# A decode block's forward and backward kernel: its instruction order planned anew, with landing times of all transfers in flight renewed at each issue

## The chip, the cores and the metric

The kernel runs on one core of a Trainium2 chip. The metric is the device time of one execution in microseconds (us); lower is better. The time before is the median of five runs.

## What is computed

The reference is a decode step (one token, batch 2) of grouped-query attention over a cache plus a bilinear gated MLP, and its gradients by `jax.vjp`. Cut to what matters:

```python
B, D, Hq, Hkv, Sk, Dh, F = 2, 576, 32, 16, 4096, 128, 4608
xn = layernorm(x)
q = (xn @ wq).reshape(B, 1, Hq, Dh)                    # each K/V head serves 2 query heads
p = softmax(q @ k_cache^T * Dh ** -0.5)                # per head, over 4096 positions
attn = (p @ v_cache).reshape(B, 1, Hq * Dh) @ wo
mlp = ((xn @ w_gate) * (xn @ w_up)) @ w_down
out = x + attn + mlp
outputs: out, and the gradients for x, k_cache, v_cache, wq, wo, w_gate, w_up, w_down
```

All arrays are bfloat16. With one token, every gradient of a cache or a weight is an outer product: it is as large as the cache or the weight itself and has to be written in full. The caches are 64 heads-by-batch pieces of 1 MB to read, and their gradients 64 pieces of 1 MB to write.

## The kernel before

The work has 16 steps. A step `s` is one group of two K/V heads (`g = s // 2`, eight groups) for one of the two batch rows. Beside the steps there are nine slices of 512 columns of the MLP (`mlp`, L666 ff.).

- **Cache loads** (`load_kv`, L926, on SP's queue): four a step, K then V for two heads, 1 MB each, into nine buffers `kv`.
- **Turning** (`turn`, DVE, L357): each cache buffer is transposed in 32x32 blocks into one of three buffers `X`, two instructions of 1024 columns each.
- **Group front** (`group_front`): L787 multiplies w_q of the group with the normalised token (20 matmuls: four heads of four 128-row blocks and one small block, which comes in a transfer of its own, L940); L820 does the same for w_o and the incoming gradient. `rep` (L804) carries the result to POOL, which builds the stationaries `W` (L1001) of the steps.
- **Attention** (`softmax`, `dscore`): scores (L1036, 32 matmuls per head), softmax with row maximum and sum through small matmuls, then `spread` (L1048, L1054), whose copy to `pp` or `dd` is what the next stages read.
- **Outer products** (`head_outer`, L1069): `BD`, a block-diagonal form of the query or gradient made by POOL (L1024, 32 times), times `pp` or `dd`. Two matmuls fill a PSUM buffer `o` (three of them); an eviction on ACT (L361) or DVE (L363) casts 128x1024 values into a stage buffer `st` (four of them). Four evictions make one 1 MB piece of a cache gradient, which SP stores (L583). `BIAS` tilts the choice between ACT and DVE.
- **Contraction** (`contract`, L1209): p with V and dscore with K from the untransposed buffers, in four parts; after the last the four `kv` buffers of the step are free for the next loads.
- **Group back** (`group_back`) after two steps: the gradients of w_q and w_o, again outer products through `st`, stored from POOL's queue (L583), with `tl` for the last 64 rows.
- **MLP slice**: loads of w_gate and w_up (POOL L959, small parts SP L962) and w_down (SP L966), then its products and three gradients stored from POOL.

Every engine runs its instructions in the order in which they stand, and so do the two queues from which transfers are issued, SP's and POOL's: an instruction that waits holds all that stands behind it. That order isn't written by hand. Each part of the work is a generator that yields what it needs (an engine for so long, a buffer of a ring, an event, a transfer); the class `Order` keeps a clock per engine with costs written in the source, and takes, among the parts that could start within `SLACK` of the earliest on an engine, the one with the lowest priority number (`PR`, with `HEAD` for steps 0 and 1 and `TAIL` for steps 14 and 15, plus `STEP` per step). The instructions are emitted in the order so found. The class `Lines` is its model of the transfers: two lines, SP's and POOL's, that share the transfer rate by packet size; `push` adds a transfer and says when it will land. Weights are loaded when a certain count of cache loads has been issued: `8*g + WQ0` and `8*g + WO0` for w_q and w_o, `MLP0 + i*MLPD` for the slices.

The clock of `Order` exists only while the program is built. On the chip, waits are semaphores that follow from what is read and written.

Of the kernel before, what the change touches and what calls it, by code (L numbers as in the profile page):

```python
# [31 lines left out]
        self.land = None  # L32


class Lines:
    def __init__(self):
        self.now, self.line = 0.0, ([], [])

    def work(self, line, until):
        while self.now < until and (line[0] or line[1]):  # L40
            busy = [q for q in line if q]
            total = sum(q[0][1] for q in busy)
            step = min(min(q[0][0] * total / q[0][1] for q in busy), until - self.now)
            for q in busy:
                q[0][0] -= step * q[0][1] / total
                if q[0][0] < 1e-9:
                    q.pop(0)
            self.now += step

    def push(self, k, at, work, packet):  # L50
        self.work(self.line, at)
        if not (self.line[0] or self.line[1]):
            if at > self.now + 0.3:
                work += DRY
            self.now = max(self.now, at)
        self.line[k].append([work, packet])
        now, line, n = self.now, tuple([list(x) for x in q] for q in self.line), len(self.line[k])
        while line[k]:
            self.work(line, self.now + 1e-6 + min(q[0][0] for q in line if q))
        end, self.now = self.now, now  # L60
        return end


class Order:
# [44 lines left out]
    def start(self, s):  # L109
        r = s.req  # L110
        if r[0] == "op":
            return max(s.ready, self.free[r[1]]), r[1]
        if r[0] == "any":
            best = None
            for e, cost, bias in r[1]:
                t = max(s.ready, self.free[e])
                if best is None or t + cost + bias < best[0]:
                    best = (t + cost + bias, t, e)
            return best[1], best[2]
        if r[0] == "wait":  # L120
            if any(e.t is None for e in r[1]):
                return None, None
            return max([s.ready] + [e.t for e in r[1]]), None
        if r[0] == "acq":
            ts = [t for t in self.slots[r[1]].values() if t is not None]
            if not ts:
                return None, None
            return max(s.ready, min(ts)), None
        if r[0] == "dma":
            return max(s.ready, self.free[r[1]]), r[1]  # L130
        if r[0] == "gate":
            if r[2] < 0:
                return s.ready, None
            e = r[1][min(int(r[2]), len(r[1]) - 1)]
            return (None, None) if e.t is None else (max(s.ready, e.t), None)
        raise ValueError(r)

    def run(self):
        while self.streams:
            cand = []  # L140
            for s in self.streams:
                t, e = self.start(s)
                if t is not None:
                    cand.append((t, s.prio, s, e))
            assert cand, "no stream can go on: %s %s" % (
                [(x.gen.__name__, x.gen.gi_frame.f_lineno, x.ready, x.req) for x in self.streams], self.slots)
            t, _, s, e = min(cand, key=lambda c: c[:2])
            if e is not None:
                t, _, s, e = min((c for c in cand if c[3] == e and c[0] <= t + SLACK[e]), key=lambda c: (c[1], c[0]))
            r = s.req  # L150
            value = None
            if r[0] in ("op", "any"):
                cost = r[2] if r[0] == "op" else next(c for x, c, _ in r[1] if x == e)
                quad = r[3] if len(r) > 3 else None
                if quad is not None and self.quad == (1 - quad, t):
                    cost = 0.12
                self.free[e] = t + cost
                if e == "PE":
                    self.quad = (quad, t + cost)
                s.ready = t + cost + self.HOP  # L160
                self.log.append((t, cost, e, s.gen.__name__))
                value = e
            elif r[0] in ("wait", "gate"):
                s.ready = t
            elif r[0] == "acq":
                slots = self.slots[r[1]]
                i = min((k for k, v in slots.items() if v is not None), key=lambda k: (slots[k], k))
                slots[i] = None
                s.ready = t
                value = i  # L170
            elif r[0] == "dma":
                self.free[e] = t + r[2]
                s.land = self.lines.push(e == "POOL", t + r[2] + LATENCY[e], r[3], r[4]) + 1.4
                s.ready = t + r[2]
                self.log.append((t, r[2], e, s.gen.__name__))
            self.advance(s, value)
# [34 lines left out]
def WAIT(*events):  # L211
    return ("wait", events)


def SET(event):
    return ("set", event)
# [10 lines left out]
def DMA(engine, cost, nbytes, row=8192):  # L227
# [3 lines left out]


NKV, NX, NGU, NWW, NST, NBD = 9, 3, 1, 5, 4, 3
MLP0, MLPD = 7, 4.12
KVSTORE = "SP"
WQ0, WO0 = -6, 0
LATENCY, DRY = {"SP": 0.6, "ACT": 0.6, "POOL": 2.0}, 0.4
BIAS = 0.37
SLACK = {"PE": 0.05, "ACT": 0, "DVE": 0, "POOL": 4.39, "SP": 3.25}
STEP = 28.0  # L240
HEAD = {"turn0": 37.0, "turn1": -35.7, "att": -22.4, "dsc": 17.6, "con": -15.0, "out0": 23.5, "front": 20.5, "back": 16.6, "W1": -1.0, "BD1": 2.3, "BD0": -12.8, "load": -30.3}
TAIL = {"turn0": -15.1, "att": -22.9, "dsc": -43.3, "con": 54.4, "out1": 30.2, "back": -0.9, "W0": 22.3, "W1": 12.9, "BD1": 41.5, "BD0": 93.7, "load": 0.2}
PR = {"turn0": 171.8, "turn1": 90.3, "att": 19.2, "dsc": -129.0, "con": 69.0, "out1": 42.8, "out0": 77.7, "front": -89.9,
      "back": 17.7, "W0": -47.7, "W1": 227.7, "BD1": -2.0, "BD0": -48.1, "mlp": -78.9, "wout": 54.1, "store": 33.6,
      "load": 262.3, "wload": -168.7, "fin": -1.5, "const": 62.9, "mload": 371.2}


def pr(name, s):
# [5 lines left out]
def kernel(  # L254
# [33 lines left out]
    NS = NG * Bq  # L288
# [281 lines left out]
    class Store:  # L570
        def __init__(self, n, out, prio):
            self.n, self.out, self.prio = n, out, prio
# [197 lines left out]


    grp = [dict(Lm=Event(), Eq=Event(), Ed=Event(), Lq=Event(), Lo=Event()) for _ in range(NG)]
    steps = [dict(done=Event(), outs=[Event(), Event()], sm=Event(), dsv=Event()) for _ in range(NS)]

    def group_front(g):
        st = grp[g]
# [323 lines left out]
    def softmax(s):  # L1100
# [47 lines left out]
        yield REL("m", m)  # L1148
        yield SPAWN(outer(s, 1, "pp", S["pp"], pp_t[S["pp"]][:, 1]), pr("out1", s))
        S["ppT"] = pp_t[S["pp"]][:]  # L1150

    def dscore(s):
        S = steps[s]
# [41 lines left out]
    def contract(s):  # L1195
        S = steps[s]
        g, b = divmod(s, Bq)
        if b == 0:
            grp[g]["oT"] = yield ACQ("oT")
        oT = oT_t[grp[g]["oT"]]  # L1200
        yield WAIT(S["sm"], Ezero)
        m = yield ACQ("m")
        ct = m_t[m]
        heads = [(S["ppT"], kvS[s][1][l], l) for l in range(G)] + [(S["ddT"], kvS[s][0][l], l) for l in range(G)]
        for part in range(4):
            yield PE(0.95)
            for c in range(8 * part, 8 * part + 8):
                for j, (rT, slot, l) in enumerate(heads):
                    nc.tensor.matmul(ct[32 * j:32 * j + 32, 0:P], lhsT=view(rT, 0, P, 4 * c + 2 * l, [[1, 32]]),  # L1209
                                     rhs=kv_t[slot][:, Dh * c:Dh * (c + 1)], start=(c == 0), stop=(c == NCH - 1))  # L1210
        for t in range(2):
            for l in range(G):
                yield REL("kv", kvS[s][t][l])
        i = yield ACQ("osb")
        e = yield EV(128)
        if e == "ACT":
            nc.scalar.activation(osb_t[i][:], ct[:, 0:P], AF.Copy, scale=oscale[:])
        else:
            nc.vector.tensor_scalar(osb_t[i][:], ct[:, 0:P], oscale[:], None, op0=ALU.mult)
        yield REL("m", m)  # L1220
        m = yield ACQ("m")
        yield PE(0.3)
        nc.tensor.matmul(m_t[m][:, 0:8], lhsT=osb_t[i][:], rhs=view(ident[:], 0, P, 0, [[32, 4], [1, 2]]),
                         start=True, stop=True)
        yield REL("osb", i)
        yield DVE(0.19)
        nc.vector.tensor_copy(view(oT[:], 0, P, b, [[GH * 32, 2], [32, GH]]),
                              m_t[m][:, 0:8].rearrange("p (t h) -> p t h", t=2))
        yield REL("m", m)
        yield SET(S["done"])  # L1230
# [148 lines left out]
```

## Time and profile before

| what | value |
|---|---|
| median of five runs | 513.48 us (509.31 to 515.99) |
| the profiled execution: its own time, its span | 513.48 us, 511.7 us |
| instructions | 19318 |
| PE, DVE, ACT, POOL busy | 377.1, 372.1, 305.2, 228.1 us |
| moved by DMA | 186.19 MB, half read and half written |
| mean granted TensorE clock | 0.667 |

The page gives busy time per engine; the span in 40 slices of 12.8 us, where a digit is the busy share in tenths; the queues; the chain of work that ended last; groups of instructions with their mean duration and the idle time before them. Line numbers are those of the kernel before. Waits name the instruction that waited and the one that released it. A DMA share of 1.00 in a stretch means that the core's 16 DMA engines were busy throughout it.

### The profile page before, as it was taken

The numbers are of one execution on the slowest core, as the hardware profiler recorded it, in microseconds if no ns is written. First come the engines' busy times: TensorE is split into PE (matmuls) and PEld (weight loads), VectorE is DVE, ScalarE is ACT, GpSimd is POOL, SyncE is SP. The second block draws the span as 40 slices with busy tenths as digits, with TensorE's granted clock in tenths as the row PEclk, the third lists the DMA queues.
The fourth block names the chain that finished last, engine by engine and source line by source line (L and its number), as shares of the span: only waits on it lengthen the run. The fifth ranks groups of instructions, "written<-read, shape, count | busy, mean of one in ns | idle before, by whom it ended". The sixth has DMA issues, their size and how long they took to land.

```text
span 511.7 us, 19318 instructions
## 1 busy us (share of the span) xinstructions
PE 377.1 (74%) x8506; PEld 246.9 (48%) x8506; DVE 372.1 (73%) x657; ACT 305.2 (60%) x463; POOL 228.1 (45%) x323
## 2 busy tenths in 40 slices
PE   0629848878787888597787776678588875896976
PEld 0417535645455464445456443444455563563544
DVE  6739958789665788769683984659776775897883
ACT  5025837575673758284783746447466664867783
POOL 6147534447424545446334362416551462256411
PEclk9997757585655667756765965557655666966775
DMA  7994889999998999999999899967999999899885
GB/s 275 402 370 185 328 327 367 409 409 407 410 397 351 341 379 374 392 420 420 393 401 411 297 417 408 412 264 295 396 377 408 410 380 385 345 378 325 341 336 215
DMA packets 34235, 186.19 MB, mean 364 GB/s; under 512 B 4156, under 2 KB 6344, under 8 KB 17768
## 3 DMA queue, kind: packets, MB, share of 16 engines
q1 hardware_dynamic: 22224, 141.25, 69.8%
q0 software_dynamic: 11920, 43.72, 22.4%
q8 instruction: 66, 1.08, 0.8%
q14 instruction: 17, 0.14, 0.1%
q10 hardware_dynamic: 8, 0.00, 0.0%
HBM read 92.48 MB, written 92.48 MB: 361 GB/s over the span
## 4 chain that ended last, share of the span: by engine, by line
PE 33%; DMA 33%; issue 11%; DVE 10%; ACT 9%; POOL 3%; SPq 1%; ACTq 0%; DVEq 0%; POOLq 0%
DMA out_dram<-st 23%; ACT st L361 8%; PE ps_o L1069 7%; PE ps_m L1209 6%; PE ps_m L1036 6%; DMA ww<-in_A_wq_dram 5%; DVE X L357 5%; DMA gu<-in_B_w_up_dram 4%; DVE st L363 2%; PE ps_m L820 2%; PE ps_o L603 2%; PE ps_m L679 1%; POOL BD L1024 1%; PE ps_o L617 1%; SPq L926 1%
## 5 line engine op out<-in xcount | busy, mean ns | idle before, releaser
L361 ACT CAST st<-ps_o 128x1024 bf16<-128x1024 f32 (+1 forms) x290 | 258.9, 946 | 124.0 <-DMA out_dram<-st 62.1
L357 DVE STREAM_TRANSPOSE X<-kv 128x1024 f32<-128x1024 f32 x128 | 154.7, 1223 | 9.9 <-PE ps_m L1036 5.0
L1024 POOL TENSOR_TENSOR BD<-vr,mask 128x2048 bf16<-128x2048 bf16 x32 | 115.2, 3599 | 43.7 <-PE ps_o L1069 24.2
L363 DVE CAST st<-ps_o 128x1024 bf16<-128x1024 f32 (+1 forms) x86 | 99.3, 1158 | 42.7 <-DMA out_dram<-st 18.8
L583 POOL DMA_DIRECT2D out_dram<-st x43 | 33.2, 772 | 99.3 <-ACT st L361 69.7
L1069 PE MATMUL ps_o<-BD,pp 32*128 32x512 bf16 x256 | 51.9, 521 | 23.2 <-ACT st L361 22.9
L1036 PE MATMUL ps_m<-X,W 128*32 128x128 bf16 x2048 | 62.8, 292 | 5.9 <-issue 2.1
L1209 PE MATMUL ps_m<-kv,pp 128*32 128x128 bf16 x1024 | 56.9, 279 | 9.4 <-issue 9.3
L1069 PE MATMUL ps_o<-BD,dd 32*128 32x512 bf16 x256 | 54.8, 512 | 9.8 <-ACT st L361 6.0
L1209 PE MATMUL ps_m<-kv,dd 128*32 128x128 bf16 x1024 | 56.6, 279 | 3.1 <-issue 3.1
L1036 PEld LDWEIGHTS <-W 128*32 128x32 bf16 x2048 | 48.2, 130 | 19.7 <-issue 15.5
L1209 PEld LDWEIGHTS <-pp 128*32 128x32 bf16 x1024 | 44.2, 126 | 15.5 <-issue 14.7
L1209 PEld LDWEIGHTS <-dd 128*32 128x32 bf16 x1024 | 44.0, 126 | 8.8 <-issue 8.8
L1001 POOL COPY W<-rep 32x16 bf16<-32x16 bf16 x128 | 24.6, 192 | 47.2 <-DVE rep L804 31.7
L357 DVE STREAM_TRANSPOSE X<-ww 128x1152 f32<-128x1152 f32 x25 | 34.3, 1371 | 5.9 <-PE ps_m L1036 3.2
L1069 PEld LDWEIGHTS <-pp 32*128 32x128 bf16 x256 | 11.2, 98 | 41.6 <-issue 38.1
L1069 PEld LDWEIGHTS <-dd 32*128 32x128 bf16 x256 | 13.0, 98 | 26.2 <-issue 21.7
L554 POOL COPY wt<-wm 64x128 bf16<-64x128 bf16 (+1 forms) x34 | 8.9, 260 | 31.0 <-DVE wm L548 30.0
L583 POOL DMA_DIRECT2D out_dram<-tl x26 | 14.5, 561 | 18.0 <-ACT tl L361 9.8
L357 DVE STREAM_TRANSPOSE X<-gu 128x1024 f32<-128x1024 f32 x18 | 22.0, 1227 | 0.3 <-PE ps_m L1036 0.3
L787 PE MATMUL ps_m<-xs,ww 128*128 128x2 bf16 x160 | 5.7, 165 | 15.7 <-DMA ww<-in_A_wq_dram 8.4
L603 PEld LDWEIGHTS <-xnr 32*128 32x128 bf16 x416 | 12.9, 119 | 7.2 <-issue 6.1
(202 smaller groups left out, 526.0 us busy)
## 6 DMA issues: line engine op xcount, KB each, us to landing
out_dram<-st SPq DMA_DIRECT2D x64, 1024.0 KB
kv<-in_A_k_cache_dram SPq DMA_DIRECT2D x32, 1024.0 KB
kv<-in_A_v_cache_dram SPq DMA_DIRECT2D x32, 1024.0 KB
out_dram<-st POOLq DMA_DIRECT2D x26, 512.0 KB, 7.2
out_dram<-st POOLq DMA_DIRECT2D x17, 576.0 KB, 9.5
ww<-in_B_w_down_dram SPq DMA_DIRECT2D x9, 576.0 KB
ww<-in_A_wo_dram POOLq DMA_DIRECT2D x8, 576.0 KB, 10.5
gu<-in_B_w_gate_dram POOLq DMA_DIRECT2D x9, 512.0 KB, 11.3
```

Source lines behind the costliest of these rows:

```text
L357: nc.vector.transpose(out, in_)
L361: nc.scalar.copy(out, in_)
L363: nc.vector.tensor_copy(out=out, in_=in_)
L554: nc.gpsimd.tensor_copy(view(Wt[:], 64 * h, 64, 0, [[dims[-1][1], n], [1, dims[-1][1]]]), view(Wm[:], 64 * h, 64, off, dims))
L583: (nc.gpsimd if engine == "POOL" else nc.sync).dma_start(dst, src)
L603: nc.tensor.matmul(o[:, aa, dc * P:(dc + 1) * P], lhsT=xnr[32 * a:32 * a + 32, dc * P:(dc + 1) * P], rhs=rhs(a), start=True, stop=True)
L820: nc.tensor.matmul(dp, lhsT=Wdy[:, e, 2 * k:2 * k + P], rhs=view(X[:], 0, P, 64 * k + e, [[D, GH], [2, 32]]), start=(k == 0 and e == 0), s ...
L1001: nc.gpsimd.tensor_copy(view(W_t[t][w][:], 32 * a, 32, 6 + 8 * a, [[G * WW, 4], [WW, G], [1, 2]]), view(rep_t[grp[g]["qs"]][:], 32 * a, 32 ...
L1024: nc.gpsimd.tensor_tensor(BD_t[i][:], view(vr_t[v][:], 0, P, 0, [[0, 16], [1, Dh]]), view(mask16[:], 0, P, 0, [[1, 16], [0, Dh]]), ALU.mult)
L1036: nc.tensor.matmul(sc[32 * cq:32 * cq + 32, :], lhsT=view(W[:], 0, P, (be * G + l) * WW + 6 - 4 * c2 - 2 * l, [[1, 32]]), rhs=view(X[:], 0 ...
L1069: nc.tensor.matmul(o[:, k, :], lhsT=pr2[32 * c4:32 * c4 + 32, :], rhs=BD[32 * c4:32 * c4 + 32, 8 * l + 4 * h2:8 * l + 4 * h2 + 4, :], star ...
L1209: nc.tensor.matmul(ct[32 * j:32 * j + 32, 0:P], lhsT=view(rT, 0, P, 4 * c + 2 * l, [[1, 32]]), rhs=kv_t[slot][:, Dh * c:Dh * (c + 1)], sta ...
```

## The change

In the planner, a transfer's landing time was a number, worked out once when the transfer was issued, with the transfers known at that moment. Now it is an object (`Landing`), and each later issue, on either line, works out anew when every transfer in flight lands; whoever asks reads the newest value (`when`). With that model another set of gates, slacks and priorities is given, and so another order of the instructions on all engines. In the program, `contract` waits in the planner for an event set at the end of `softmax` (`spread`, after the copy to `pp`) in place of the one set before `spread` is planned (`sm`). Work, tiles, buffers and queues per transfer stay.

```diff
+class Landing:
+    def __init__(self, work, packet):
+        self.work, self.packet, self.t = work, packet, None
+
+def when(x):
+    return x.t if isinstance(x, Landing) else x
...
     def push(self, k, at, work, packet):
-        self.work(self.line, at)
+        self.run(at)
         if not (self.line[0] or self.line[1]):
             if at > self.now + 0.3:
                 work += DRY
             self.now = max(self.now, at)
-        self.line[k].append([work, packet])
-        now, line, n = self.now, tuple([list(x) for x in q] for q in self.line), len(self.line[k])
-        while line[k]:
-            self.work(line, self.now + 1e-6 + min(q[0][0] for q in line if q))
-        end, self.now = self.now, now
-        return end
+        item = Landing(work, packet)
+        self.line[k].append(item)
+        now, line, left = self.now, self.line, [[(x, x.work) for x in q] for q in self.line]
+        self.line = tuple(list(q) for q in line)
+        self.run()
+        self.now, self.line = now, line
+        for q in left:
+            for x, w in q:
+                x.work = w
+        return item
...
-            return max([s.ready] + [e.t for e in r[1]]), None
+            return max([s.ready] + [when(e.t) for e in r[1]]), None
...
-                s.land = self.lines.push(e == "POOL", t + r[2] + LATENCY[e], r[3], r[4]) + 1.4
+                s.land = self.lines.push(e == "POOL", t + r[2] + LATENCY[e], r[3], r[4])
...
-MLP0, MLPD = 7, 4.12
+MLP0, MLPD = 8, 3.49
-WQ0, WO0 = -6, 0
+WQ0, WO0 = -2, -2
-BIAS = 0.37
-SLACK = {"PE": 0.05, "ACT": 0, "DVE": 0, "POOL": 4.39, "SP": 3.25}
+BIAS = 0.15
+SLACK = {"PE": 0.11, "ACT": 0.21, "DVE": 0.31, "POOL": 0.93, "SP": 5.91}
-HEAD = {"turn0": 37.0, "turn1": -35.7, "att": -22.4, "dsc": 17.6, "con": -15.0, "out0": 23.5, ...}
+HEAD = {"turn0": -96.9, "turn1": -63.0, "att": -34.6, "dsc": -63.3, "con": 2.5, "out1": -1.3, ...}
-TAIL = {"turn0": -15.1, "att": -22.9, "dsc": -43.3, "con": 54.4, "out1": 30.2, ...}
+TAIL = {"turn1": 6.7, "att": -0.5, "dsc": -47.3, "con": 173.2, "out1": -11.9, ...}
-PR = {"turn0": 171.8, "turn1": 90.3, "att": 19.2, "dsc": -129.0, "con": 69.0, ..., "load": 262.3, ...}
+PR = {"turn0": 615.2, "turn1": 519.1, "att": -36.4, "dsc": -131.1, "con": 373.1, ..., "load": 650.0, ...}
...
+        yield SET(S["spread"])
...
-        yield WAIT(S["sm"], Ezero)
+        yield WAIT(S["spread"], Ezero)
```

What it does to the order, place by place. SP's queue has 168 places in both; the first 16 are the same. The loads of the nine MLP slices begin at places 12, 24, 44, 71, 84, 104, 125, 142, 153 before and at 12, 23, 37, 54, 66, 80, 96, 109, 119 after. The last cache load stands at place 149 before and 150 after. On POOL, the ten clears of buffers stand ahead of the loads of group 1's weights; they were mixed before. On PE, L787 of group 1 stood ahead of the second half of step 0's softmax, and stands now after it, after three outer products and after the first half of step 0's dscore. ACT evicts 17 pieces of the weight gradients fewer, DVE 17 more; the cache gradients' 256 evictions are shared as before, 184 and 72.

More of the change, by code (lines that the diff above doesn't have):

```diff
@@ L37, in __init__, with run @@
         self.now, self.line = 0.0, ([], [])
[L39 to L43, printed above, removed]
-            for q in busy:
-                q[0][0] -= step * q[0][1] / total
-                if q[0][0] < 1e-9:
+    def run(self, until=None):
+        while (self.line[0] or self.line[1]) and (until is None or self.now < until):
+            busy = [q for q in self.line if q]
+            total = sum(q[0].packet for q in busy)
+            step, first = min(((q[0].work * total / q[0].packet, k) for k, q in enumerate(busy)))
+            ends = until is None or step <= until - self.now
+            step = step if ends else until - self.now
+            for q in busy:
+                q[0].work -= step * q[0].packet / total
+            self.now += step
+            for q in busy:
+                if q[0].work < 1e-9 or ends and q is busy[first]:
+                    q[0].t = self.now + 1.4
                     q.pop(0)
-            self.now += step
     def push(self, k, at, work, packet):
-        self.work(self.line, at)
+        self.run(at)
         if not (self.line[0] or self.line[1]):
@@ L122, in start @@
                 return None, None
-            return max([s.ready] + [e.t for e in r[1]]), None
+            return max([s.ready] + [when(e.t) for e in r[1]]), None
         if r[0] == "acq":
-            ts = [t for t in self.slots[r[1]].values() if t is not None]
+            ts = [when(t) for t in self.slots[r[1]].values() if t is not None]
             if not ts:
@@ L134, in start @@
             e = r[1][min(int(r[2]), len(r[1]) - 1)]
-            return (None, None) if e.t is None else (max(s.ready, e.t), None)
+            return (None, None) if e.t is None else (max(s.ready, when(e.t)), None)
         raise ValueError(r)
@@ L166, in run @@
                 slots = self.slots[r[1]]
-                i = min((k for k, v in slots.items() if v is not None), key=lambda k: (slots[k], k))
+                i = min((k for k, v in slots.items() if v is not None), key=lambda k: (when(slots[k]), k))
                 slots[i] = None
@@ L233 @@
 NKV, NX, NGU, NWW, NST, NBD = 9, 3, 1, 5, 4, 3
-MLP0, MLPD = 7, 4.12
+MLP0, MLPD = 8, 3.49
 KVSTORE = "SP"
-WQ0, WO0 = -6, 0
+WQ0, WO0 = -2, -2
 LATENCY, DRY = {"SP": 0.6, "ACT": 0.6, "POOL": 2.0}, 0.4
-BIAS = 0.37
-SLACK = {"PE": 0.05, "ACT": 0, "DVE": 0, "POOL": 4.39, "SP": 3.25}
+BIAS = 0.15
+SLACK = {"PE": 0.11, "ACT": 0.21, "DVE": 0.31, "POOL": 0.93, "SP": 5.91}
 STEP = 28.0
[L241 to L245, printed above, removed]
+HEAD = {"turn0": -96.9, "turn1": -63.0, "att": -34.6, "dsc": -63.3, "con": 2.5, "out1": -1.3, "front": 86.3, "back": 152.3, "W0": 79.2, "W1": 113.2, "BD1": 32.1, "load": 16.8}
+TAIL = {"turn1": 6.7, "att": -0.5, "dsc": -47.3, "con": 173.2, "out1": -11.9, "out0": 27.4, "front": 423.6, "W0": 21.5, "BD1": -20.6, "BD0": 13.1, "load": -7.5}
+PR = {"turn0": 615.2, "turn1": 519.1, "att": -36.4, "dsc": -131.1, "con": 373.1, "out1": 249.7, "out0": 254.3, "front": -120.6,
+      "back": 33.0, "W0": 336.5, "W1": 402.2, "BD1": 480.8, "BD0": 19.3, "mlp": -146.2, "wout": -154.9, "store": 349.0,
+      "load": 650.0, "wload": 29.8, "fin": 213.7, "const": 44.3, "mload": 912.6}
 def pr(name, s):
@@ L772 @@
     grp = [dict(Lm=Event(), Eq=Event(), Ed=Event(), Lq=Event(), Lo=Event()) for _ in range(NG)]
-    steps = [dict(done=Event(), outs=[Event(), Event()], sm=Event(), dsv=Event()) for _ in range(NS)]
+    steps = [dict(done=Event(), outs=[Event(), Event()], sm=Event(), spread=Event()) for _ in range(NS)]
     def group_front(g):
```

## The prediction

> **What bounds the kernel now.** I read the page first: busy shares, then the forty slices.
>
> ```profile
> PE 377.1 (74%) x8506; PEld 246.9 (48%) x8506; DVE 372.1 (73%) x657; ACT 305.2 (60%) x463; POOL 228.1 (45%) x323
> ...
> DMA  7994889999998999999999899967999999899885
> GB/s 275 402 370 185 328 327 367 409 409 407 410 397 351 341 379 374 392 420 420 393 401 411 297 417 408 412 264 295 396 377 408 410 380 385 345 378 325 341 336 215
> DMA packets 34235, 186.19 MB, mean 364 GB/s; under 512 B 4156, under 2 KB 6344, under 8 KB 17768
> ```
>
> No engine is above 74%, and the DMA row is mostly 9: transfers set the time, except where the row falls. So I cut the span into 5 us stretches (sixth value after the core: DMA share, then GB/s) and summed what is missing to a share of 1.
>
> ```profile
> 35.00:40.00 5.00, 4.08 (x112) 2.75 (x112) 4.81 (x7) 3.38 (x6) 3.12 (x4) 1.00 0.77 253
> 40.00:45.00 5.00, 3.90 (x70) 2.78 (x72) 4.96 (x13) 3.10 (x5) 3.33 (x8) 0.95 0.27 112
> 45.00:50.00 5.00, 5.00 (x157) 4.05 (x159) 4.73 (x6) 2.48 (x4) 4.08 (x6) 0.50 0.78 316
> 50.00:55.00 5.00, 4.31 (x116) 3.33 (x109) 4.24 (x7) 2.21 (x3) 3.62 (x5) 0.87 0.49 177
> ...
> 225.00:230.00 5.00, 4.57 (x62) 2.56 (x60) 4.33 (x9) 4.43 (x9) 3.44 (x2) 0.50 1.03 430
> ...
> 335.00:340.00 5.00, 1.94 (x36) 0.45 (x21) 1.29 (x3) 2.59 (x4) 0.36 (x1) 0.50 0.53 217
> 340.00:345.00 5.00, 5.00 (x136) 3.32 (x140) 3.90 (x5) 3.36 (x4) 1.92 (x9) 0.51 0.62 231
> 345.00:350.00 5.00, 4.45 (x117) 2.93 (x105) 4.86 (x11) 3.77 (x6) 1.43 (x2) 1.00 0.42 165
> ```
>
> The dry time is 39.8 us: 3.2 in the first 5 us, 8.5 from 35 to 55, 17.8 from 55 to 440 (7.2 of it in the three last rows), 10.3 after 440 (3.4 in 505 to 510, 1.7 in the last stub). The other 471.9 us move 186.19 MB at 394 GB/s. Only the dry time is to be won: the floor of any order is near 480.
>
> Then, what the dry stretches follow: two rows of the waits of the whole span (engine line, releaser: us in total, times, longest), and two of PE's timeline in the opening (start, length, the idle time before in brackets):
>
> ```profile
> ACT st L361 <- DMA out_dram<-st: 62.1, 22, 9.1
> ...
> DVE st L363 <- DMA out_dram<-st: 18.8, 8, 5.8
> ```
>
> ```profile
> 25.62 0.24 PE L787 MATMUL ps_m<-xs,ww 128*128 128x2 bf16 x4 [0.35 <-ACT vr L361]
> ...
> 34.22 0.58 PE L787 MATMUL ps_m<-xs,ww 128*128 128x2 bf16 x16 [8.36 <-DMA ww<-in_A_wq_dram]
> ```
>
> The timeline: PE stands 8.4 us at L787, the query product of group 1, after four of its matmuls; the fifth needs the small w_q piece that SP issued at 6.48 behind seven cache loads. All of step 0 that stands later in PE's order waits with it, and the first cache stores leave at 42.94. The waits: evictions stand 80.9 us for a stage buffer whose store has not landed. ACT waits 5.2 us for one until 337.4, and the dry rows 335 to 350 follow. An order built on landing times that are too early makes both: it puts an instruction that waits ahead of some that need not.
>
> **The change, part by part.** *The landing model and the added wait.* They exist while the program is built. Matmuls, evictions and transfers are the same in number, 167 issues on SP in both. The contraction's new event names the copy of pp, which its matmuls read in any case: nothing on the chip, nothing queued behind it. 0 us.
>
> *Opening.* SP's order is the same to place 14, so the w_q piece lands at 34.2 again. POOL now issues group 1's w_q and w_o after ten clears, near 7.5 us instead of 3.8 and 4.9; the first w_q, ahead on the same queue, lands at 12.1 (PEld's wait), so that ring stays full: 0, and at most the 3 us of delay if it ran dry. In PE's new order L787 of group 1 comes after the softmax of step 0, three outer products and half of its dscore. From before's durations: exp's sum ready 26.0, then the row sum, reciprocal, scaling, spread and copy, 2.2 us as at 34.66 to 36.86: 28.2. BD ends at 25.72+3.60 = 29.3; three evictions (1.02, 1.21, 1.02) are through by 32, and PE waits only the last 1.5 us or so. After 34.2: L787 0.58, second dscore half 1.04, the fourth product 0.4, eviction 1.02, some 0.5 of hops: first store at 37.8, second at 40 (before 42.94 and 46.1). Then DVE rules until the contraction lets buffers go: three transposes of 1.22, two of 1.37, two evictions of 1.21 and fourteen small ones of 3.5 in all, 12.3 us from 35.9, so 48.2, one small product and the last contraction part 0.97: cache loads near 50, before 51.5. In DMA terms: two stores fill to 44, the third comes at 47.3, the loads at 50: dry 4 instead of 8.5. I take -4; ends 0 (another wait takes the place) and -8.4 (the whole stall).
>
> *Middle.* SP now carries the cache loads in runs of four between runs of two to four stores; single loads between stores fall from 5 to 2. w_q of a group is gated at cache load 8g-2 (was 8g-6), w_o at 8g-2 (was 8g): weight buffers are held for about four loads less. Of the 17.8 dry us, 11.4 follow at once on a wait for a store's landing in the chain (2.6 at 70 to 80, 7.2 at 335 to 350, 1.7 at 430 to 440). Those are what truer landing times can remove; a new order has some of its own. The trace can't show how many. Ends -17.8 and +18 (as many again); I take -8, nearest to the 11.4.
>
> *ACT's and DVE's shares.* Six more evictions of 1024 columns (1.21), eight of 576 (0.75) and a few small ones go to DVE, six osb scalings (0.33) leave it: DVE +11 us, ACT -9. DVE stays under 383 of some 497, 77%: 0, hidden by transfers; up to 11 if DVE were the bound.
>
> *End.* Before, the last MLP slice is loaded after the last cache load (SP places 153 to 155); in the new order at 119 to 121. After the last cache load only 13 cache stores (13.6 MB), two groups' weight gradients (2.4 MB) and loads in flight (some 4 MB) remain, 20 MB against 23.4 that the trace moves from 440 on, and no MLP chain. What is left then is 45 evictions on ACT, 41 us (33 of 1.02, 12 of 0.65), and 23 with ten transposes and the small steps on DVE, about 47, less than 20 MB at 394 GB/s, 51 us. The 5.1 dry us of the very end (final products, output rows) stay; of the other 5.2 I take -3; ends 0 and -5.
>
> **Two rules against it.** The Trainium skill, "DMA: Bandwidth & Descriptors", section "Where 436 GB/s comes from", says that HBM-to-SBUF transfers are bound by the HBM side at about 358 GB/s per core. By that 186.19 MB need 520 us, more than the span, and no order wins anything. The row 225 to 230 has 430, and the mean is already 364: the measurement decides, and the 394 of the busy stretches is mine. "TensorE: Matmul & The Clock Gate", section "What's actually happening", says that idleness throttles PE and activity releases it, so filling the stall would make PE faster. Here the clock is 1.00 in 30 to 35, where PE is busy 0.78 of 5 us, and 0.50 in 45 to 50, where it is busy throughout: the row says denser work is slowed. It costs little either way: 32 score matmuls took 1.04 us at clock 1.00 (at 18.33) and 0.88 to 0.98 at 0.50. By the rule up to 1 us less in the opening, by the row 0; I take 0.
>
> **Sum.** Span 511.7-4-8-3 = 496.7; around it 1.8 (513.48-511.7): 498.5. The profiled execution's time is the median of the five.
>
> **Rivals.** *A, only the opening and the end:* new waits for stage buffers replace the old ones; -4-3 gives 506.5. For: there are still four stage buffers shared by both store queues. Against: those waits are where the old landing times erred.
> *B, it doesn't do what it says:* the chip's landings stay as far from the renewed ones as from the old, for each dry spell removed another comes: 513.5. Against: the 8.4 us stall is passed by in PE's order whatever the model is worth.
> *C, slower:* cache loads stand in SP's line behind runs of stores, each of which waits for its evictions; SP already waits long so:
>
> ```profile
> SPq L583 <- DVE st L363: 140.5, 40, 11.1
> SPq L583 <- ACT st L361: 69.9, 31, 7.4
> ```
>
> Three stores in flight cover 7.8 us (2.6 each at 400 GB/s); once they are out, K and V come late. There are 14 such batches. At 1.1 us of dry time each the 15 are eaten, at 1.4 it is slower by 1%; at 2 us it is +28-15 = 526.5. For: a store held late now holds four loads together. Against: most of SP's waits lie in stretches with DMA share 1.
>
> **Chances and range.** Forecast 0.5 (488 to 508), A 0.14 (502 to 511), B 0.12 (508 to 517), C 0.24 (514 to 535). About 1%, 508.3 to 518.6, is what a measurement can tell. Faster: 0.49+0.10+0.01 = 0.60; same: 0.01+0.04+0.11+0.04 = 0.20; slower: 0.20. The range for 8 in 10 is 487 to 521, leaving out the upper part of C and the lower tail.
>
> **What would show it.** Right: no long PE wait at L787's line before the first outer products, first cache store before 39, dry time from 35 to 55 about 4; waits for landings of stores on ACT and DVE well under 80.9; dry time from 55 to 440 about 10; no MLP work in the last 40 us; the time over the DMA share's sum still near 472. Wrong: the busy stretches below 385 GB/s, more dry time in the middle than 17.8, or SP's runs of loads preceded by dry DMA.

## The result, and the profile after

The changed kernel takes 507.26 us (median of 24 runs, 502.22 to 511.12), the old one beside it 512.41 (45 runs): ratio 0.9905, 95% interval 0.9884 to 0.9925. That is 5 us, a third of the 15 forecast. (Ratios leave disturbed runs out, in e4 half of them, so a few differ by some tenths of a per cent from those of the medians.) The profiled execution of the changed kernel took 505.19 us with a span of 503.3. Its lines stand 17 or 18 lower in the source than before: L361 is L378, L363 L380, L583 L600, L787 L804, L1036 L1053, L1069 L1086, L1209 L1227.

Its page, busy shares and transfers:

```profile
PE 361.9 (72%) x8506; PEld 238.6 (47%) x8506; DVE 390.4 (78%) x665; ACT 300.0 (60%) x455; POOL 228.1 (45%) x323
...
DMA  7997999999899899999999989999899997999886
GB/s 273 402 377 291 386 407 420 409 401 418 301 402 400 331 378 346 333 413 399 416 400 388 404 332 401 337 405 392 276 422 391 384 368 277 396 419 376 327 345 253
```

DVE has 18 us more than before (11 were forecast), ACT 5 less. The evictions and scalings that moved to DVE come to 11.6 us, as forecast; the rest is mainly two small casts (L846) of some 3 us each, where the median of the eight is 0.17, and three constants at the start of 2.4 to 2.5 us where they took 0.5 to 0.6. Why these take longer, no run shows. Summed in 5 us stretches as in the prediction, the dry time stands so:

| stretch | before | forecast | after |
|---|---|---|---|
| 0 to 5 | 3.2 | 3.2 | 3.2 |
| 35 to 55 | 8.5 | 4.5 | 3.3 |
| 55 to 440 | 17.8 | 9.8 | 17.0 |
| from 440 | 10.3 | 7.3 | 9.9 |
| in all | 39.8 | 24.8 | 33.5 |

The two profiled executions lie 8 us apart, 3 more than the medians. Of the 8.4 us between their spans 6.3 are dry time; the remaining stretches took 469.8 us instead of 471.9, at 396 GB/s.

The opening did what was forecast. PE's and SP's timelines after (start, length; the idle time before in brackets):

```profile
30.94 0.27 PE L804 MATMUL ps_m<-xs,ww 128*128 128x2 bf16 x4
...
34.09 0.59 PE L804 MATMUL ps_m<-xs,ww 128*128 128x2 bf16 x16 [2.89 <-DMA ww<-in_A_wq_dram]
```

```profile
37.27 9.57 SPq L600 DMA_DIRECT2D out_dram<-st  x3
48.88 0.34 SPq L943 DMA_DIRECT2D kv<-in_A_k_cache_dram  x1
```

The w_q piece lands when it did, but PE now stands 2.9 us for it instead of 8.4. The first store leaves at 37.3 (forecast 37.8, before 42.9), the loads go on at 48.9 (forecast near 50, before 51.5).

The middle did not. The waits for store landings, from the waits of the whole span (us in total, times, longest), and SP's:

```profile
ACT st L378 <- DMA out_dram<-st: 45.8, 19, 5.4
...
DVE st L380 <- DMA out_dram<-st: 22.0, 9, 4.7
```

```profile
SPq L600 <- DVE st L380: 165.4, 44, 12.8
SPq L600 <- ACT st L378: 96.8, 32, 15.5
```

They are 67.8 us instead of 80.9. SP stands longer behind evictions (262 us instead of 210). What the dry stretches look like has changed more than how many there are (each row: length; busy us of PE, PEld, DVE, ACT and POOL; clock; DMA share; GB/s. So the DMA share is the last value but one, and not the sixth, as the prediction counts):

```profile
335.00:340.00 5.00, 4.75 (x130) 2.98 (x126) 4.09 (x8) 3.77 (x7) 2.26 (x5) 0.50 1.02 426
340.00:345.00 5.00, 4.17 (x66) 3.10 (x64) 3.57 (x9) 2.84 (x3) 1.87 (x4) 0.50 1.02 404
345.00:350.00 5.00, 2.05 (x64) 1.34 (x52) 2.45 (x5) 1.67 (x4) 0.87 (x3) 0.50 1.03 413
350.00:355.00 5.00, 4.46 (x154) 3.71 (x143) 5.00 (x9) 2.71 (x4) 4.12 (x2) 0.50 0.77 292
...
415.00:420.00 5.00, 5.00 (x87) 2.73 (x88) 4.44 (x7) 3.65 (x6) 1.53 (x8) 0.50 0.65 265
```

The stretch 335 to 350, which held 7.2 us of dry time, is full. Others are dry in its place, and there the engines work: PE is busy 5.00 of 5 us (second value) and DVE 4.44 (fourth) in the last row, DVE 5.00 in the row before. From 345 to 350 it is the other way round: full transfers, engines at less than half. I cut 55 to 440 into stretches of 1 us and averaged those with a DMA share under 0.85: 38 before, with DVE busy 0.72, and 36 after, with DVE busy 0.91 (PE 0.82 and 0.83, ACT 0.74 and 0.68).

### The profile page after: what moved, and what is told of

Read it like the earlier page. It is cut to its first block, busy times and chain, and to the rows that moved or that the text cites. A ratio compares the mean times of both kernels' runs of the same rounds, so it can differ in the third digit from the quotient of the medians.

```text
span 503.3 us, 19348 instructions
## 1 busy us (share of the span) xinstructions
PE 361.9 (72%) x8506; PEld 238.6 (47%) x8506; DVE 390.4 (78%) x665; ACT 300.0 (60%) x455; POOL 228.1 (45%) x323
## 2 busy tenths in 40 slices
DMA packets 34235, 186.19 MB, mean 370 GB/s; under 512 B 4156, under 2 KB 6344, under 8 KB 17768
## 5 line engine op out<-in xcount | busy, mean ns | idle before, releaser
L378 ACT CAST st<-ps_o 128x1024 bf16<-128x1024 f32 (+1 forms) x276 | 248.4, 950 | 119.2 <-DMA out_dram<-st 45.8
L380 DVE CAST st<-ps_o 128x1024 bf16<-128x1024 f32 (+1 forms) x100 | 112.8, 1132 | 55.3 <-DMA out_dram<-st 22.0
L600 POOL DMA_DIRECT2D out_dram<-st x43 | 33.0, 769 | 76.4 <-ACT st L378 32.9
L1053 PE MATMUL ps_m<-X,W 128*32 128x128 bf16 x2048 | 60.3, 284 | 7.5 <-issue 5.3
L1086 PE MATMUL ps_o<-BD,pp 32*128 32x512 bf16 x256 | 48.4, 505 | 16.4 <-ACT st L378 10.4
L1086 PE MATMUL ps_o<-BD,dd 32*128 32x512 bf16 x256 | 48.7, 502 | 9.4 <-ACT st L378 6.1
L1053 PEld LDWEIGHTS <-W 128*32 128x32 bf16 x2048 | 46.3, 125 | 19.1 <-issue 17.2
L1227 PE MATMUL ps_m<-kv,pp 128*32 128x128 bf16 x1024 | 51.8, 262 | 2.5 <-issue 2.2
L1227 PE MATMUL ps_m<-kv,dd 128*32 128x128 bf16 x1024 | 51.7, 263 | 1.4 <-issue 1.4
L1227 PEld LDWEIGHTS <-pp 128*32 128x32 bf16 x1024 | 39.6, 118 | 18.8 <-issue 18.0
L1227 PEld LDWEIGHTS <-dd 128*32 128x32 bf16 x1024 | 39.2, 118 | 1.5 <-issue 1.5
L600 POOL DMA_DIRECT2D out_dram<-tl x26 | 14.6, 563 | 31.2 <-ACT tl L378 25.4
L1086 PEld LDWEIGHTS <-pp 32*128 32x128 bf16 x256 | 10.8, 97 | 30.0 <-issue 24.2
L1086 PEld LDWEIGHTS <-dd 32*128 32x128 bf16 x256 | 11.3, 98 | 22.8 <-issue 17.2
L374 DVE STREAM_TRANSPOSE X<-gu 128x1024 f32<-128x1024 f32 x18 | 21.2, 1209 | 0.4 <-PE ps_m L1053 0.4
L634 PE MATMUL ps_o<-dyr,R 32*128 32x288 bf16 x64 | 10.1, 391 | 15.6 <-ACT st L378 14.7
L696 PE MATMUL ps_m<-gu,xs 128*32 128x128 bf16 x360 | 10.4, 270 | 10.0 <-DMA gu<-in_B_w_up_dram 7.4
## 6 DMA issues: line engine op xcount, KB each, us to landing
kv<-in_A_k_cache_dram SPq DMA_DIRECT2D x32, 1024.0 KB, 11.6
ww<-in_A_wo_dram POOLq DMA_DIRECT2D x8, 576.0 KB, 13.7
```

The lines of the kernel that those rows point to most:

```text
L374: nc.vector.transpose(out, in_)
L378: nc.scalar.copy(out, in_)
L380: nc.vector.tensor_copy(out=out, in_=in_)
L600: (nc.gpsimd if engine == "POOL" else nc.sync).dma_start(dst, src)
L634: nc.tensor.matmul(o[:, aa, 0:HD2], lhsT=lhs(a), rhs=dyr[32 * a:32 * a + 32, k * HD2:(k + 1) * HD2], start=True, stop=True)
L696: nc.tensor.matmul(ug[32 * a:32 * a + 32, 1 - w, :], lhsT=xs[:, dc if dc < 4 else 4 + w, :], rhs=gu[:, FS * k + P * a:FS * k + P * (a + 1) ...
```

## The experiments

The forecast's theory: transfers set the time, waits for landings dry them in the middle, and truer landing times remove those. A rival: the engines' own ordered work is about as long as the transfers, so that a wait removed soon meets the next engine. Another: DVE alone is the limit, through its 18 us more. Where a recorded expectation names a theory by a letter or a number, the figures beside it say what it holds. "Whole" means that everything is stored.

**The opening alone**, from both sides. Everything else keeps its recorded order; the cut tells the moves in words.

```diff
 e3, PE's order of before (48 rows moved):
-L787 of group 1; softmax of step 0, second half; outer products; dscore
+softmax of step 0, second half; 3 outer products; dscore, half; L787 of group 1
 e4, PE's order of the changed kernel:
-softmax of step 0: row sum; ...; L804 of group 1
+L804 of group 1; softmax of step 0: row sum; ...
```

> The kernel before with its order kept instruction for instruction (PE 48 of 16783 rows moved, DVE and ACT 3 and 1, SP none) but for one place: the query product of group 1 and what hangs on it come after the softmax of step 0, three outer products and half of its dscore. Theory 1 (the whole gain is the opening's): opening dry time from 8.4 to about 3.5 us, first cache store near 37.5, and the time 5 us lower, about 507.5. Theory 2 (the opening is caught up with later, since transfers already saturate there; the gain comes from many places): dry time falls in the opening and rises later by as much, time unchanged, 512.

> The changed kernel with its order kept (PE 43 of 16783 rows moved, SP and POOL none) but for one place: the row sum of step 0's softmax waits in PE's order for the query product of group 1, as before the change. Theory 1: 8 us of PE stall come back, opening dry about 8, time about 512, all of the gain lost. Theory 2: about 507, unchanged.

e3: 509.80, ratio 0.9952 (0.9925 to 0.9978), against 513.60 in the same batch. e4: 511.91, ratio 0.9922 (0.9890 to 0.9955). In e4's trace 35 to 55 is dry for 8.3 us again, and the whole span for 39.8, as before the change. In e3 the first store leaves at 40.6 instead of the expected 37.5, and 35 to 55 is dry for 4.8. By the medians the opening is worth 3.8 put in, 4.7 taken out, most of the gain; by the ratios 2.5 and 1, a half or a fifth of it. So its place is shown, and its share of the 5 us is not settled.

**Model and numbers apart.**

```diff
 e1: the changed kernel
-MLP0, MLPD = 8, 3.49        # and WQ0, WO0, BIAS, SLACK, HEAD, TAIL, PR
+MLP0, MLPD = 7, 4.12        # all as before
 e2: the kernel before
-MLP0, MLPD = 7, 4.12
+MLP0, MLPD = 8, 3.49        # all as in the changed kernel
```

> The changed planner (landing times renewed) with the gates, slacks, BIAS and priorities of before. Its order already has the group 1 product late. Theory 1: about 507, as the changed kernel, with dry time in the middle near 17 as in both. If truer landing times also help the middle (my forecast's term), middle dry time near 10 and time near 500.

> The old landing model with the new gates, slacks, BIAS and priorities (and the added wait). Its order has the group 1 product early again. Theory 1: the opening's stall is back, about 512 or more. If the new numbers carry the gain: 507.

e1: 514.91, ratio 1.0049 (1.0027 to 1.0071). e2: 524.13, ratio 1.0208 (1.0163 to 1.0253). Either half alone loses, and both at the end: 20.6 and 21.2 us dry from 440 on, where both kernels have 10. e1's middle, with 13.9, is better than either's; but e3, with the old model and the old numbers, has 14.4, so this alone says nothing for the model. I tried to mend its end with the slices' gates:

```diff
 e12: e1
-MLP0, MLPD = 7, 4.12
+MLP0, MLPD = 8, 3.49
```

> The renewed landing model with the constants of before (514.9, with 20.6 us of dry time after 440), and of the new constants only the gates of the MLP slices (8 and 3.49 in place of 7 and 4.12), so that the last slice comes earlier. If the late slices make the loss of the end, the dry time after 440 falls to 10 or so: 502 to 507, better than either kernel because its middle is dry for 13.9 only. If priorities of the last steps make it: 512 to 517, still near 20 of dry time after 440.

518.79, ratio 1.0117 (1.0072 to 1.0163), 23.0 us dry from 440. The edit missed its aim: the last slice's loads stand at SP's places 152 to 154 still (151 to 154 in e1), since a gate only permits, and the priorities decide. That late slices make the loss of the end stays untested.

**Lighter engines.**

```diff
 e5: half the turning
-t32(pairs(X_t[x][:, 2048 * h:2048 * h + 2048]), ...)
+t32(pairs(X_t[x][:, 2048 * h:2048 * h + 1024]), ...)
 e6: half the contraction
-for c in range(8 * part, 8 * part + 8):
+for c in range(8 * part, 8 * part + 8, 2):
 e8: 17 of DVE's 45 weight gradient evictions go to ACT
 e10: e5 and e6
```

> The changed kernel with the same order, but each of the 128 cache transposes on DVE turns only half of its columns (the scores are then taken over half-filled tiles; six clears of the other halves are added at the start). DVE loses about 75 of 390 us. Theory D (what dries the middle is DVE: it is busy 0.91 in the 36 dry microseconds there, 0.77 in the others): dry time from 55 to 440 from 17 to under 8, time about 495. Theory L (late landings of stores and full stage buffers dry it, DVE is busy only because it runs in bursts): dry time stays above 13, time above 503.

> The changed kernel with the same order, but the contraction takes every second chunk of the cache (1024 of its 2048 matmuls are left out). PE loses about 50 of 362 us. Theory P (PE, 0.83 busy in the dry microseconds, is what holds the bursts): dry time of the middle under 8, time about 495. Theory D: nearly nothing, dry time above 13, time above 503. Theory L: the same as D.

> The changed kernel with the same order, but 17 of the 45 weight-gradient evictions that DVE has are given to ACT at the same place, evenly over the span: DVE about -12 us, ACT +11, as many as before the change. Theory D: the dry time of the middle falls by 3 to 5 us and the time to 503 to 505. Theory L: unchanged, 507.

> The changed kernel with the turning and the contraction both halved (half of each turned buffer and every second chunk of the contraction left out): DVE about 75 us lighter, PE about 50. Either alone gave 501.2 and 496.6 against 507.3. If the engines take turns at holding the end, the two gains add or more: 490 or below, toward the 472 of the transfers with some 11 of opening and end, 483. If PE alone holds it: 495 to 498, as without the lighter DVE.

e5: 501.15, ratio 0.9735 (0.9668 to 0.9801). e6: 496.58, 0.9677 (0.9618 to 0.9736). e8: 507.79, 0.9907 (0.9874 to 0.9940). e10: 491.68, 0.9578 (0.9515 to 0.9640). DVE fell by 62 us in e5 (a turn of half the width takes 0.70 us, a whole one 1.23) and the time by 6.1: DVE doesn't hold the end alone, and e8 says so too: moving its extra evictions to ACT changes nothing. The middle is dry for 13.3 us in e5, 11.6 in e6, 15.1 in e8 and 6.5 in e10: neither engine alone brings it under 8, both together do. The gains of e5 and e6 nearly add by the medians (6.1 + 10.7, 15.6 measured; 8.7, 11.7 and 16.8 by the ratios), and e10 misses its "490 or below" by 2. Meanwhile the waits for store landings rise, from 67.8 us to 96.3 in e10:

```profile
ACT st L378 <- DMA out_dram<-st: 64.6, 31, 5.4
DVE st L380 <- DMA out_dram<-st: 31.7, 16, 5.9
```

So in these runs the dry time follows the engines' work and not these waits. By the forecast's theory none of these runs was to move the time by much. What makes e6 faster is not taken apart: it leaves out matmuls, but also lets the `kv` buffers go sooner, and PE's busy time stays (see the last section).

**Small stores.** One line takes most of the store traffic away, and with it most waits for landings. It leaves seven eighths of each cache gradient unwritten.

```diff
 e7 (changed kernel), e9 (before), e14 (e4), e15 (e1), e16 (e2), e11 (e5), e13 (e6)
-[(oviews[t][b, G * g + l], st[:], 1 << 20)]
+[(oviews[t][b, G * g + l][:, 0:512], st[:, 0:512], 1 << 20)]
```

> The changed kernel with the same order, but each of the 64 cache gradient stores moves one eighth of its piece (seven eighths of both cache gradients are not written): 127 MB instead of 186, 323 us at 394 GB/s. If transfers alone set the time and dry stretches are waits for landings (theory L), near 400. If the order of the engines' work itself is a floor close under the present time (theories D and P: bursts of work between dependent batches), 450 to 480.

> The order of before, with only one eighth of each cache gradient piece stored (seven eighths of the cache gradients are left unwritten). The changed kernel lost 32 us by the same edit (507.3 to 475.0). If two limits lie side by side (transfers near 472, the engines' ordered work near 475) and the orders differ only in the opening, whose stall for w_q hangs on loads and stays: the same loss, some 478 to 483. By the forecast's reading the old order suffers more from waits for store landings, so it gains more from their absence, by the 8 us of the middle: 470 to 474. If the old order is worse for the engines themselves, apart from any landing: above 487.

> The changed kernel's order with only the row sum of step 0's softmax put back behind the query product of group 1, and seven eighths of the cache gradients unwritten. If the opening counts in full where stores are small, so that the rest of the new order is the longer one by some 7: 479 to 481 beside 475.0. If small stores hide the opening, so that the rest of the two orders differs by 2 only: 474 to 476.

> Renewed landing model with the constants of before (514.9 with whole stores), seven eighths of the cache gradients unwritten. If the model is what cuts the cost of landings (40.5 in before, 32.3 in the changed kernel): 514.9-32=483. If the new constants cut it: 514.9-40=475.

> Old landing model with the new constants (524.1 with whole stores), seven eighths of the cache gradients unwritten. If the model cuts the cost of landings: 524.1-40=484 or less, since the old model keeps the full cost. If the new constants cut it: 524.1-32=492.

| order | whole | small stores | ratio of the small to before, interval | difference |
|---|---|---|---|---|
| before | 512.4 | 472.6 | 0.9216 (0.9167 to 0.9264) | 39.8 |
| changed | 507.3 | 475.0 | 0.9261 (0.9215 to 0.9307) | 32.3 |
| changed, opening put back | 511.9 | 479.5 | 0.9351 (0.9301 to 0.9401) | 32.4 |
| new model, old numbers | 514.9 | 492.8 | 0.9616 (0.9560 to 0.9671) | 22.1 |
| old model, new numbers | 524.1 | 497.0 | 0.9680 (0.9617 to 0.9743) | 27.1 |

The page of the changed order with small stores, and of the old one:

```profile
PE 361.0 (76%) x8506; PEld 238.7 (51%) x8506; DVE 389.6 (82%) x665; ACT 300.2 (64%) x455; POOL 228.1 (48%) x323
...
DMA  7993796899399656699959974797983965681122
```

```profile
PE 356.4 (76%) x8506; PEld 237.2 (51%) x8506; DVE 371.4 (79%) x657; ACT 304.4 (65%) x463; POOL 228.1 (49%) x323
...
DMA  7993687949897829996498698927699696847332
```

A third of the bytes is gone (127.47 MB instead of 186.19), the DMA row falls to 1 in places, the waits for landings fall from 67.8 to 21.8 us (changed) and from 80.9 to 19.8 (before), and still 475 us (changed) and 473 (before) remain with no engine above 82%. In the changed order transfers idle for 132.5 us of it, and PE and DVE wait some 17 us for loads (8.1 for w_q, 7.1 for w_up, 2.1 for K). So it is mostly the length of the engines' work in its order, and it lies beside the 472 us that the transfers need. This is the reading that the forecast lacked.

The table says three things. The opening is worth 4.6 us where most waits for landings are gone (479.5 to 475.0; the runs of the two don't overlap). The rest of the new order is then 7 us *longer* than the old (479.5 against 472.6), while with whole stores it is level or better (by 0.5 by the medians, by 4 by e4's ratio). A part of the 7 may still be the opening: 35 to 55 is dry for 14.6 us in e14 and 11.8 in e9. And e9's number is the one that the forecast's theory gave: the old order gains 8 us more from small stores. That is tempting: 8 us of landings won, 7 lost to the engines' order. But the difference isn't a cost that adds. It shrinks as the order itself grows longer, whichever model made it (e15 and e16 gave 22 and 27 where either theory wanted 32 or 40): longer engine work covers more of the transfers. Between the old model's two rows it falls by 12.7 over 24.4 us; on that line an order of 479.5 would have 36 and one of 492.8 would have 29, and the new model's have 32.4 and 22.1. Truer landings may thus be worth 4 to 7, a hint from a line through two points.

> The changed kernel with seven eighths of the cache gradients unwritten and half of the turning left out. Small stores alone: 475.0, with DVE busy 389.6 us and PE 361.0. If DVE alone holds the engines' time there: 475 less most of its 75 us, 400 to 425. If PE alone: 471 to 475. If they alternate, or the limits of buffers between them count: between, 440 to 465.

> The changed kernel with seven eighths of the cache gradients unwritten and every second chunk of the contraction left out, so that PE has some 50 us less. Small stores alone: 475.0; small stores with half the turning (DVE 61 us lighter): 470.8. If PE's own work sets the 475: 475-45=430, up to 440. If round trips between the engines set it: 460 to 472, as with the lighter DVE.

e11: 470.81, ratio 0.9148 (0.9080 to 0.9216); e13: 466.37, ratio 0.9091 (0.9039 to 0.9143). With 61 us less on DVE 4.2 are won, with half the contraction 8.6. Neither engine alone sets the 475. So DVE's 18 us more are hardly the reason for the 7 either: 61 us less bring 4.2. That leaves the turns that they take at one another, and the buffers between them; no run here shows which of these.

**A fifth stage buffer**, with all bytes; for the room, two turned buffers in place of three. e17 keeps the changed order, e18 plans anew.

```diff
-NKV, NX, NGU, NWW, NST, NBD = 9, 3, 1, 5, 4, 3
+NKV, NX, NGU, NWW, NST, NBD = 9, 2, 1, 5, 5, 3
```

> The changed kernel's order kept, with five stage buffers in place of four and two turned buffers in place of three (for the room). All is computed and stored. If waits for the landing of stores hold the time in the middle: those 67.8 us fall by half, dry time from 55 to 440 falls from 17.0 to 10 or less, 500. If the engines' own round trips hold it: the waits fall, and the time stays or rises, since score products now wait for the turning: 506 to 515.

> The same two counts of buffers given to the planner, which finds its own order with them; all constants are those of the changed kernel. If landings hold the time: 495 to 503, better than the kept order. If round trips hold it: 505 to 520.

e17: 551.54, ratio 1.0780 (1.0689 to 1.0872); e18: 517.16, ratio 1.0143 (1.0081 to 1.0204). From the waits of e18:

```profile
ACT st L378 <- DMA out_dram<-st: 14.9, 7, 3.6
DVE X L374 <- PE ps_m L1053: 13.7, 19, 1.7
DVE st L380 <- DMA out_dram<-st: 9.0, 4, 3.7
```

The waits for landings fell from 67.8 to 23.9 us, and the middle is dry for 20.0 instead of 17.0. (In e17 they are 38.2, and 40.8 us are dry.) The missing turned buffer has its price (13.7 here, 33.0 for the same wait in e17), so this doesn't measure what the landings cost alone; it shows that fewer of those waits don't by themselves keep the transfers busy. A fifth stage buffer beside three turned ones was not tried.

Beside each other, with everything stored:

| order | waits for landings, ACT and DVE | dry from 55 to 440 | time |
|---|---|---|---|
| e10, half turning and contraction | 96.3 | 6.5 | 491.7 |
| before | 80.9 | 17.8 | 512.4 |
| changed | 67.8 | 17.0 | 507.3 |
| e1, new model, old numbers | 41.0 | 13.9 | 514.9 |
| e18, five stage buffers | 23.9 | 20.0 | 517.2 |

## Why the forecast was wrong

- **"I take -4" for the opening**: right in place, and by the dry time in size: it fell by 5.2. The first store and the loads came within about a microsecond of the forecast times. In time e3, e4 and e14 give 1 to 4.7.
- **"Those are what truer landing times can remove ... I take -8", the middle**: this step failed. Dry time fell by 0.8. The 11.4 us were read off the chain as following a wait for a landing, and booked as what goes when that wait goes. The waits fell by 13.1, and dry stretches with DVE at 0.91 took the place of those at 0.72. Over the runs the dry time doesn't follow these waits (the table above): in e10 they are the longest and the middle is dry the least, in e18 the other way round. It fell to 6.5 where DVE and the contraction had less to do. The last release in a chain says what came last, not what would have come next; what stood behind each single wait, no run shows. Nor is it excluded that truer landings won 4 to 7 us which the longer order of the engines lost again.
- **"Only the dry time is to be won: the floor of any order is near 480"**: true as a bound, wrong as a reading of what holds the time. No engine above 74% was taken to mean that engines follow. Small stores leave 473 to 475 us, mostly engine work in its order.
- **"DVE +11, ACT -9 ... 0"**: the size was 18 and 5, of which 11.6 on DVE is the work that moved. e8 shows no price for the evictions' place. But that the order as a whole costs nothing was wrong: without the opening it is up to 7 longer where stores are small. Which part of the new order makes the 7 stays open.
- **"-3" for the end**: -0.4. The slices are gone from the end, as forecast, but from 460 to 485 the transfers are dry for 5.2 us with PE, DVE and ACT each busy 82 to 88% of the time. The step compared each engine's sum with the transfers, one at a time; three engines so busy at once fit a stretch in which they wait for each other, which is not shown.
- **Rivals**: A (only the opening and the end, 506.5) came within a microsecond of the result, and in part by luck: the reason that it named, new waits for stage buffers, is not what the trace shows (those waits fell by 13.1; engine work came in their place), and its -3 for the end was -0.4. The middle went as B said, another dry spell for each removed; whether for B's reason, landings no better known than before, no run shows. C's mechanism, stores held late on SP, is there (262 us of waits for evictions, 52 more), but mostly while transfers run.
- **The order as one thing**: the forecast gave the landing model no share of its own. e1 and e2 show that the model without its numbers, or the numbers without their model, loses 2.5 and 10.7 us by the ratios: these numbers suit the model beside which they stand.

No experiment beat the changed kernel with all its work done; e8 is level with it.

## What to carry to other kernels

Busy shares of 74% and a full DMA row don't say that only transfers limit: take most of one resource's work away and see what length remains, for where two limits of about equal length lie side by side, a wait removed at one soon meets the other. Before a wait in a chain is booked as gain, see over a few variants whether the dry time follows that wait: here it fell where the engines had less to do, while the waits grew. Move a single stall with everything else replayed, as e3 and e4 do, to price it apart from a new order.

## What was unexpected of the hardware

Half the contraction didn't make PE's busy time shorter. The changed kernel, then e6 (groups: busy, mean ns, idle before):

```profile
L1227 PE MATMUL ps_m<-kv,pp 128*32 128x128 bf16 x1024 | 51.8, 262 | 2.5 <-issue 2.2 <-DVE qd L807 0.2
...
L1086 PE MATMUL ps_o<-BD,dd 32*128 32x512 bf16 x256 | 48.7, 502 | 9.4 <-ACT st L378 6.1 <-DVE st L380 1.8 <-DVE kv L1278 1.1
```

```profile
L1086 PE MATMUL ps_o<-BD,dd 32*128 32x512 bf16 x256 | 54.2, 551 | 6.2 <-ACT st L378 2.8 <-issue 1.6 <-DVE kv L1278 1.1
...
L1227 PE MATMUL ps_m<-kv,pp 128*32 128x128 bf16 x512 | 34.5, 284 | 1.8 <-issue 1.0 <-DVE accx L782 0.6 <-DVE qd L807 0.2
```

A contraction matmul takes 284 ns instead of 262, an outer product 551 instead of 502. The contraction's rows lose 34.6 us (103.5 to 68.9), all other matmul rows gain 18.5, and as a union PE is busy 362.9 us (361.9 before the edit). (The profile models where a matmul ends, so these are rough.) The granted clock fell from 0.678 to 0.629 in the profiled pair, and from 0.655 to 0.619 by the medians of the runs; with small stores e13 shows the same (364.7 instead of 361.0 us, clock 0.617 instead of 0.691, medians 0.635 and 0.686). Of the 50 us that the expectations of e6 and e13 took off PE, none shows in its busy time, though the kernel became 11 and 9 us shorter. The cut came with a slower clock for the rest in both pairs; why the clock falls, no run shows. The prediction's reading that denser work is slowed is a tendency at most: in the 5 us stretches before, the clock has a mean of 0.57 where PE is busy for 95% or more and 0.73 where it is busy for under 60%, but the row 335 to 340 has 0.50 with PE busy for 1.94 of 5 us, and in e6 less PE work came with the lower clock. A cut of PE work can't be booked at the duration that its rows show.
